# AdaLN block with memory-recurrent attention, forward and backward: the rows of a segment's out-projection and of its dH summed and turned off TensorE

## Chip, cores and metric

One Trainium2 chip, one core of it. The metric is the device time of one execution in microseconds (us), as the median of several runs. Engines in the profile: PE is TensorE (PEld its weight loads), DVE is VectorE, ACT is ScalarE, POOL is GpSimd, SP is SyncE, which issues most DMAs.

## What is computed

The output of the block and, by the vector-Jacobian product for `grad_out`, the gradients of its eleven differentiable inputs. Everything comes in as bfloat16. S = 2048 rows of D = 512; 32 heads of 128; 64 segments of 32 rows, each behind a memory of 8 rows; F = 1792.

```python
def _A_ref(x, mem0, Wq, Wk, Wv, Wo, seg_len):
    ...
    mem = mem0
    for s in range(n_seg):
        xs = x[:, s * seg_len:(s + 1) * seg_len, :].copy()
        h = jnp.concatenate([mem, xs], axis=1)          # 8 + 32 rows
        q = jnp.einsum('btd,dhe->bhte', h, Wq)
        ...                                             # k, v, masked softmax p
        o = jnp.einsum('bhqk,bhke->bhqe', p, v)
        o = jnp.einsum('bhte,hed->btd', o, Wo)
        mem = o[:, :M, :].copy()                        # M = 8: the next segment's memory
        outs.append(o[:, M:, :])
...
sa, ca, ga, sb, cb, gb = ...                            # from silu(c) @ w_mod
h = _layernorm(x, axis=-1) * (1 + ca) + sa
x = x + ga * _A_ref(h, A_mem0, A_Wq, A_Wk, A_Wv, A_Wo, A_seg_len)
h = _layernorm(x, axis=-1) * (1 + cb) + sb
x = x + gb * _B_ref(h, B_w_gate, B_w_up, B_w_down)      # (sigmoid(h Wg) * (h Wu)) Wd
```

A segment can't start its projections before the first 8 rows of the out-projection of the segment before it are there. Backward, a segment needs the first 8 rows of dH of the segment behind it. These are the two recurrences of the kernel.

## The kernel before

The instruction order on the engines follows the program text, which is written out by hand and pinned (`self.pin`). The stages, with their places in the span:

- Phase 2 (55 to 960 us): the forward recurrence, 64 segments s, in groups of four (s4 = s % 4), 14.0 to 14.9 us each.
- Phase 3 (968 to 1470 us): the gated unit, forward and backward, by tiles of 128 rows.
- Phase 4 (1475 to 2440 us): the backward recurrence, s from 63 to 0, 14.5 to 15.3 us each.
- Phase 5 (2440 us to the end): the weight gradients, products over all rows of all segments, and dx.

*The hand-over of phase 2.* A product in this kernel has D on the partitions. The out-projection of the first 32 rows of a segment (8 memory rows and 24 others) is `pair_mm` (L218 to L223): for each of 16 pairs of heads four matmuls side by side, each in its own 32-column tile of the array, so that `at_ps` holds four partial blocks, two partials of two column halves, [128, 256]. `split_pair` makes of it a bf16 part `hi` (ACT, L230) and the rest `lo` (DVE, L232); `sum_pair` (L235 to L242) adds the partial blocks and turns them with 8 small TensorE products against a 0/1 matrix (`foldhalf`), into `at_ft`, [128 of D, 4, 32 rows]. ACT copies its first 8 columns of each block into `hT_next` (L1022), which the next segment's K and Q projections (`pass_ps<-Wk,hT`, L257) read. The same rows also go to DRAM for phases 3 and 5: `store_rows` (L330) casts `at_ft` (DVE, `at_tb`, L333), and, one pass later through a list `later`, turns it on TensorE (`at_tp`, L337), copies it (DVE, `at_rb`, L339) and stores it (POOL DMA to `AOA`, L343).

*The last 8 rows of a segment.* They are collected for four segments (`TailRows`, tiles `ao_tail`) and projected in two pieces of 24 and 8 heads at s4 = 3 by `col_mm` (L215, products of 512 columns, `ao_tps`), then split (`fold_split`, L314 and L315, `ao_b_hi`, `ao_b_lo`), summed (`fold_sum`, L325, `ao_b_ft`) and stored in the same way.

*What stands between at_ps and the next projection.* Filler, put there by hand: passes of projections for rows that don't hang on the recurrence (`b_pieces`, slots "f1" and "f2", `pass_ps<-Wk,hb` and `Wq,hb`), a product that writes the causal mask into the next scores (`mask_mm`, L783), the tail's pieces (`tail.chunk`), and some products of the modulation.

*The hand-over of phase 4* is built alike: `dht_pairs` fills `dhq_ps` (64 products of 256 columns, then four with the folded rest `dST` of `dh_ps`, L223), `split_pair` makes `dh_hi` and `dh_lo`, `sum_pair` `dh_ft`, ACT copies into `dyT` (L1936), and the next segment's pass over WoT (`pass_ps<-WoT,dyT`, L257) reads it. The rows go to `DHA` through `dh_tb`, `dh_tp`, `dh_rb`. Its tail (`dh_tps`) has three operands of 32 heads, in pieces of (16, 24, 8, 8, 16, 8, 16) heads. `proj_b` (`pass_ps<-WoT,dyb`) is the filler, and `turn_b`, eight TensorE transposes of `RBd`, stands there at s4 = 1.

*PSUM.* Phase 2's pool has five shared slots (tag "p") and one more ("b", for the tail); phase 4's shared pool has six.

*Readers.* `load_x_rows` loads 128 rows of `AOA` or `DHA`/`DHB` for phases 3 and 5, by four or eight DMAs of whole 1 KB rows; in phase 5 `p5_second` (`dyrows`) and the load of `hrows` bring the memory rows of all segments, by two DMAs each.

## Time and profile before

| | |
|---|---|
| median of 3 runs | 2995.98 us |
| lowest, highest | 2993.12, 3000.86 us |
| profiled execution: span from first to last instruction (core 0) | 2991.0 us; no time of its own outside the span is recorded |
| granted TensorE clock, mean | 0.996 |
| PE, PEld busy | 2932.8 us (98%), 1839.9 us (62%) |
| DVE, ACT, POOL busy | 1612.4 us (54%), 1271.8 us (43%), 1197.2 us (40%) |

"Busy" counts the time in which at least one instruction of the engine runs; matmuls overlap, so the duration of one (273 ns for 256 columns) is longer than the distance to the next. In lines of a group, `out<-in xcount` gives tile names and the number of instructions; in a timeline, the columns are start and length in us, engine, line, operation, `out<-in` with shapes, and in brackets how long the engine stood before it and what ended that. L223 is line 223 of the kernel before.

### The profile page before, as it was taken

The numbers are of one execution on the slowest core, as the hardware profiler recorded it, in microseconds if no ns is written. First come the engines' busy times: TensorE is split into PE (matmuls) and PEld (weight loads), VectorE is DVE, ScalarE is ACT, GpSimd is POOL, SyncE is SP. The second block draws the span as 40 slices with busy tenths as digits, with TensorE's granted clock in tenths as the row PEclk, the third lists the DMA queues.
The fourth block names the chain that finished last, engine by engine and source line by source line (L and its number), as shares of the span: only waits on it lengthen the run. The fifth ranks groups of instructions, "written<-read, shape, count | busy, mean of one in ns | idle before, by whom it ended". The sixth has DMA issues, their size and how long they took to land.

```text
span 2991.0 us, 105890 instructions
## 1 busy us (share of the span) xinstructions
PE 2932.8 (98%) x43975; PEld 1839.9 (62%) x44049; DVE 1612.4 (54%) x3679; ACT 1271.8 (43%) x3057; POOL 1197.2 (40%) x2456
## 2 busy tenths in 40 slices
PE   6999999999999999999999999999999999999999
PEld 3666666666665544445677777777777754445454
DVE  5566656666655788833456665566566532222230
ACT  2555555555555533312355555555555520011111
POOL 2454555555545222221344444444444422333321
PEclk8999999999999999999999999999999999999999
DMA  9898888889889899998699999999999997766574
GB/s 310 222 223 211 214 217 217 213 214 215 217 218 277 211 230 226 229 290 278 200 251 251 251 253 243 250 250 250 255 255 250 254 281 245 242 207 214 178 245 144
DMA packets 836438, 703.05 MB, mean 235 GB/s; under 512 B 536643, under 2 KB 708851, under 8 KB 835061
## 3 DMA queue, kind: packets, MB, share of 16 engines
q1 hardware_dynamic: 710756, 486.09, 65.5%
q0 software_dynamic: 54640, 148.90, 15.7%
q10 hardware_dynamic: 70560, 61.28, 6.5%
q8 instruction: 347, 5.69, 0.8%
q14 instruction: 135, 1.10, 0.1%
HBM read 294.99 MB, written 276.35 MB: 191 GB/s over the span
## 4 chain that ended last, share of the span: by engine, by line
PE 87%; issue 5%; DMA 3%; DVE 2%; POOL 1%; ACT 1%; SPq 1%; DVEq 0%; POOLq 0%; ACTq 0%
PE pass_ps L257 14%; PE gps L2180 9%; PE dh_ps L215 8%; PE pass_ps L659 5%; PE g_ps L1810 5%; PE gps5o L2195 4%; PE dhq_ps L223 4%; PE at_ps L223 4%; PE mm L1291 3%; PE dh_tps L215 3%; PE gps L1470 3%; PE turn_ps L829 2%; PE mm L1266 2%; PE mm L1251 1%; PE tps L1727 1%
## 5 line engine op out<-in xcount | busy, mean ns | idle before, releaser
L2180 PE MATMUL gps<-rows,hrows 128*128 128x512 bf16 (+2 forms) x2125 | 415.6, 355 | 1.8
L2180 PEld LDWEIGHTS <-hrows 128*128 128x128 bf16 x2160 | 211.3, 98 | 204.5
L61 ACT ACTIVATE ot<-gps 128x512 bf16<-128x512 f32 (+3 forms) x75 | 41.3, 550 | 362.2 <-PE gps L2180 229.1
L1855 POOL COPY dOst<-RAd 96x512 bf16<-96x512 bf16 x128 | 75.3, 613 | 297.8 <-DVE RAd L63 297.8
L1038 POOL TENSOR_TENSOR Pst<-Pst,rden 120x1408 bf16<-120x1408 bf16 x63 | 159.9, 2538 | 77.8 <-issue 49.6
L659 PE MATMUL pass_ps<-Wv,hT 128*32 128x512 bf16 (+2 forms) x2304 | 187.2, 358 | 0.0
L63 DVE CAST ot<-gps 128x512 bf16<-128x512 f32 (+3 forms) x76 | 48.1, 633 | 247.0 <-PE gps L2180 169.9
L2184 POOL DMA_DIRECT2D out_dram<-ot x108 | 81.5, 755 | 249.1 <-DVE ot L63 141.9
L257 PEld LDWEIGHTS <-hT 128*32 128x32 bf16 x4096 | 114.8, 97 | 103.9 <-issue 5.7
L63 DVE CAST Vst<-pass_ps 96x512 bf16<-96x512 f32 x128 | 87.3, 682 | 107.0 <-ACT RBv L61 98.5
L215 PE MATMUL dh_ps<-WvT,dVT 128*32 128x512 bf16 x2048 | 133.3, 380 | 1.7
L659 PE MATMUL pass_ps<-Wv,hb 128*32 128x512 bf16 (+2 forms) x636 | 128.7, 353 | 0.0
L257 PE MATMUL pass_ps<-Wq,hT 128*32 128x512 bf16 x2048 | 123.9, 383 | 4.8 <-DMA Wq<-in_A_Wq_dram 4.8
L257 PE MATMUL pass_ps<-Wk,hT 128*32 128x512 bf16 x2048 | 123.2, 382 | 2.5 <-POOL hT L549 1.1
L223 PE MATMUL at_ps<-Wo,OT 128*32 128x256 bf16 x4096 | 123.9, 273 | 0.7 <-DMA Wo<-in_A_Wo_dram 0.6
L257 PE MATMUL pass_ps<-WoT,dyT 128*32 128x256 bf16 (+1 forms) x3072 | 122.5, 308 | 0.9 <-ACT dyT L1936 0.9
L223 PE MATMUL dhq_ps<-WqT,dQT 128*32 128x256 bf16 x4096 | 122.9, 273 | 0.0
L215 PE MATMUL dh_ps<-WkT,dKT 128*32 128x512 bf16 x2048 | 122.3, 380 | 0.0
L794 POOL DMA_DIRECT2D Vst<-RBv x192 | 99.9, 526 | 55.6 <-ACT ET L841 34.4
L2195 PE MATMUL gps5o<-WoT,rows 128*128 128x512 bf16 x548 | 120.6, 379 | 1.0 <-DMA rows<-OSR 0.4
L223 PEld LDWEIGHTS <-dQT 128*32 128x32 bf16 x4096 | 109.7, 97 | 15.8
L315 DVE TENSOR_TENSOR dST<-dh_ps,dST 128x512 bf16<-128x512 f32 x64 | 44.3, 692 | 129.9 <-ACT dST L314 129.9
(471 smaller groups left out, 6991.2 us busy)
## 6 DMA issues: line engine op xcount, KB each, us to landing
OSR<-Ost SPq DMA_DIRECT2D x64, 352.0 KB
OT<-OT SPq DMA_DIRECT2D x64, 352.0 KB
PS<-Pst SPq DMA_DIRECT2D x64, 352.0 KB
Pst_l<-PS SPq DMA_DIRECT2D x64, 352.0 KB
OT_l<-OT SPq DMA_DIRECT2D x64, 352.0 KB
DVR<-rows_x POOLq DMA_DIRECT2D x64, 352.0 KB, 6.3
DKR<-rows_x POOLq DMA_DIRECT2D x64, 352.0 KB, 5.7
DQR<-rows_x POOLq DMA_DIRECT2D x64, 352.0 KB, 3.4
```

The costliest lines, as they stand in the source:

```text
L63: return nc.vector.tensor_copy(out, in_)
L215: self.nc.tensor.matmul(ps[32 * j:32 * j + 32, :], lhsT=lhsT, rhs=w, start=(n < 4), stop=(n >= total - 4), tile_position=(0, 32 * j))
L223: nc.tensor.matmul(ps[32 * j:32 * j + 32, :], lhsT=x[k], rhs=w[k][:, 256 * d:256 * d + 256], start=(n == 0), stop=(n == total - 1), tile_p ...
L257: self.nc.tensor.matmul(ps[32 * j:32 * j + 32, :], lhsT=lhs(c), rhs=rhs, start=(c == 0), stop=(c == DC - 1), tile_position=(0, 32 * j))
L659: nc.tensor.matmul(ps[32 * j:32 * j + 32, o * E:(o + n) * E], lhsT=lhsT, rhs=wc[:, 3 * a + hl:3 * (a + n - 1) + hl + 1:3, :], start=(c == ...
L794: nc.gpsimd.dma_start(Vst[96 + 8 * j:104 + 8 * j, :], rb[32 * j + o:32 * j + o + 8, :])
L1038: nc.gpsimd.tensor_tensor(Pst[0:120, :, :], Pst[0:120, :, :], rden[:, :].unsqueeze(2).to_broadcast([120, G, 128]), op=ALU.mult)
L1291: nc.tensor.matmul(hp[:], lhsT=xT[:, fc, :], rhs=wT[:, fc, :], start=(n == 0), stop=(n == 2 * FC - 1))
L1470: nc.tensor.matmul(ps[:], lhsT=h2r[:, j, c * 128:(c + 1) * 128], rhs=xr[:, j, :], start=(j == 0), stop=(j == NT - 1))
L1810: nc.tensor.matmul(ps[:, j, 0:w], lhsT=lh[:, g * GW:(g + 1) * GW], rhs=rh[:, g * GW:g * GW + w], start=True, stop=True)
L2180: nc.tensor.matmul(ps[:, 0:ng * E], lhsT=hrows[:, tp_, c * 128:(c + 1) * 128], rhs=rows[:, tp_, 0:ng * E], start=(tp_ == 0), stop=(tp_ == ...
L2195: nc.tensor.matmul(pss[gg][:], lhsT=rows[:, t, gg * E:(gg + 1) * E], rhs=dyrows[:, t, :], start=(n == 0), stop=(n == NTP - 1))
```

## The change

The four partial blocks are laid out differently (`pair_mm`: partitions 0 to 63 hold the first operand's products, 64 to 127 the second's, and columns are dealt to the blocks in runs of 32, by a rearranged moving operand). `fold_rows` then adds them off TensorE: ACT copies the lower half to SBUF in f32, and two VectorE additions write `rows`, [128, 128] bf16, four column blocks by 32 rows. `turn_rows` turns the sixteen 32x32 blocks in one VectorE transpose, and a VectorE copy moves the 8 needed columns of each block into `hT_next` or `dyT_next`. `put_rows` stores `rows` to DRAM as they are, so the row scratch (`AOM`, `AOB`, `DHM`, `DHB`) holds the columns of D in another order. Its readers undo that: `load_x_rows` and `mem_rows` by DMAs of 256-byte pieces, `blocks` as a permuted access in a VectorE multiply, an ACT copy (`dhn5`, `hrows`) or a moving operand (`dy_rows`, 4 of 20 row tiles). `split_pair`, `sum_pair`, `fold_sum`, `store_rows` and the list `later` are gone.

The tails use `pair_mm` too (256 columns, pairs of heads), in pieces of (8, 24) at s4 = 2 and 3, and (16, 24, 8, 24, 8, 16) in phase 4; `ao_tps` takes a shared PSUM slot. The filler is dealt anew: in phase 2 each of s4 = 0, 1, 2 gets six steps of `b_pieces` (s4 = 2: four and a tail piece), all three mask products stand before the hand-over, and in phase 4 `turn_b` moves to the middle of the segment with s4 = 0.

Cut to its core (four leading spaces and some context taken off):

```diff
@@ -219,30 +218,36 @@
     nc = self.nc
     for j in range(4):
-        d, k = j // 2, j % 2
-        nc.tensor.matmul(ps[32 * j:32 * j + 32, :], lhsT=x[k], rhs=w[k][:, 256 * d:256 * d + 256], start=(n == 0),
-                         stop=(n == total - 1), tile_position=(0, 32 * j))
-def split_pair(self, pool, ps, name):
+        k, d = j // 2, j % 2
+        rhs = w[k].rearrange("p (b a h x) -> p h a b x", b=4, a=2, h=2)[:, d]
+        nc.tensor.matmul(ps[32 * j:32 * j + 32, :], lhsT=x[k], rhs=rhs, start=(n == 0), stop=(n == total - 1),
+                         tile_position=(0, 32 * j))
+def fold_rows(self, pool, ps, name):
     nc = self.nc
-    hi = pool.tile([128, 256], BF16, name=name + "_hi", tag="hi0", bufs=1)
-    nc.scalar.activation(hi[:], ps[:], AF.Copy)
-    lo = pool.tile([128, 256], BF16, name=name + "_lo", tag="lo0", bufs=1)
-    nc.vector.tensor_tensor(lo[:], ps[:], hi[:], op=ALU.subtract)
-    return hi, lo
-def sum_pair(self, psp, parts, name, tag, between=None):
-    ft = psp.tile([128, self.cfg.DC, 32], F32, name=name + "_ft", tag=tag)
-    for i in range(2):
-        if i and between is not None:
-            between()
-        for c in range(self.cfg.DC):
-            self.nc.tensor.matmul(ft[:, c, :], lhsT=parts[i][:, (c % 2) * 128:(c % 2) * 128 + 128],
-                                  rhs=self.foldhalf[:, c // 2, :], start=(i == 0 and c == 0), stop=(i == 1),
-                                  skip_group_check=True)
-    return ft
+    half = pool.tile([128, 256], F32, name=name + "_half", bufs=1)
+    nc.scalar.activation(half[64:128, :], ps[64:128, :], AF.Copy)
+    rows = pool.tile([128, 128], BF16, name=name + "_rows")
+    for a in range(2):
+        nc.vector.tensor_tensor(rows[64 * a:64 * a + 64, :], ps[0:64, 128 * a:128 * a + 128],
+                                half[64:128, 128 * a:128 * a + 128], op=ALU.add)
+    return rows
+def turn_rows(self, pool, rows, name, to):
+    nc = self.nc
+    t = pool.tile([128, self.cfg.DC, 32], BF16, name=name + "_turned")
+    nc.vector.transpose(t[:].rearrange("p c t -> p (c t)"), rows[:])
+    nc.vector.tensor_copy(to, t[:, :, 0:self.cfg.M])
+def put_rows(self, dram, rows):
+    self.nc.gpsimd.dma_start(dram.rearrange("i r y -> (i r) y"), rows[:])
+def blocks(self, ap, plain):
+    return ap.rearrange("p (b i x) -> p b i x" if plain else "p (i b x) -> p b i x", b=4, i=4)
...
@@ -315,41 +320,6 @@
-def fold_sum(self, psp, parts, name, tag, pair=()):
-def store_rows(self, psp, pool, ft, dram, name, tag, then=None):
-def pop_later(self):
...
@@ -361,8 +331,9 @@
     nc, T, M = self.nc, self.cfg.T, self.cfg.M
     q = q or nc.sync
     for s4 in range(4):
-        q.dma_start(dst[s4 * T:s4 * T + 24, :], a[4 * j + s4, M:32, :])
-        q.dma_start(dst[s4 * T + 24:(s4 + 1) * T, :], b[j, 8 * s4:8 * s4 + 8, :])
+        for r0, r1, src in ((0, 24, a[4 * j + s4, :, M:32, :]), (24, T, b[j, :, 8 * s4:8 * s4 + 8, :])):
+            q.dma_start(dst[s4 * T + r0:s4 * T + r1, :].rearrange("r (i y) -> r i y", i=4),
+                        src.rearrange("i r y -> r i y"))
...
@@ -630,8 +603,8 @@
             P = lambda x, a, n, eng: (lambda: proj_b(x, a, n, eng))
             T_ = lambda x: (lambda: turn_b(x))
-            return {(0, "f1"): [P("k", 0, 4, "dve")], (1, "f1"): [P("k", 4, 4, "dve")], (1, "f2"): [P("q", 0, 2, "act")],
-                    (2, "turn"): [T_("k")], (2, "f1"): [P("q", 2, 4, "dve")], (2, "f2"): [P("q", 6, 2, "act")],
+            return {(0, "f1"): [P("k", 0, 4, "dve")], (0, "f2"): [P("k", 4, 2, "act")], (1, "f1"): [P("k", 6, 2, "act")],
+                    (1, "f2"): [P("q", 0, 4, "dve")], (2, "turn"): [T_("k")], (2, "f1"): [P("q", 4, 4, "dve")],
                     (3, "turn"): [T_("q")]}
...
@@ -968,9 +934,6 @@
             den(2, or2)
             if s4 == 3:
                 p1(s // nseg_t + P1_AHEAD, 4)
-            early = s4 == 0 and len(self.later) > 1
-            if early:
-                self.pop_later()
             more = list(range(NP)) if s + 1 < NS else []
             if more:
                 mask_mm(more.pop(0))
@@ -980,16 +943,13 @@
             fill(s4, "turn")
             if s == NS - 1:
                 turn_v(2)
-            if more and s4 < 2:
+            if more:
                 mask_mm(more.pop(0))
             ott(0)
             if more:
                 mask_mm(more.pop(0))
             ott(1)
             ott(2)
-            if not early:
-                self.pop_later()
-            self.pop_later()
             if s == NS - 1:
                 nc.gpsimd.dma_start(self.w_down, io["B_w_down"].rearrange("(fc p) d -> p fc d", p=128))
@@ -1005,21 +965,21 @@
                 first_tile[6]()
             if s + 1 < NS:
                 tails_in("kq", s + 1)
-            parts = self.split_pair(sb2, at_ps, "at")
+            rows = self.fold_rows(sb2, at_ps, "at")
+            if hT_next is not None:
+                self.turn_rows(sb2, rows, "at", hT_next[:, :, 0:M])
+            self.put_rows(self.AOM[s + 1], rows)
             tail.collect(s4, [OT])
             nc.sync.dma_start(self.OT[s], gl3(OT))
             fill(s4, "f1")
             if s == NS - 1:
                 first_tile[7]()
-            if s4 == 3:
+            if s4 >= 2:
                 tail.chunk()
             if s == NS - 1:
                 turn_p(0)
                 first_tile[8]()
-            ft = self.sum_pair(psp, parts, "at", "p", (lambda: mask_mm(more.pop(0))) if more else None)
-            if hT_next is not None:
-                nc.scalar.activation(hT_next[:, :, 0:M], ft[:, :, 0:M], AF.Copy)
             fill(s4, "f2")
             if mod_r:
                 mod_r.pop()()()
...
@@ -1027,10 +987,7 @@
                 load, products = self.mod_rest(psp, sb2, mod_at.index(s + 1))
                 load()
                 mod_r.append(products)
-            if s4 == 3:
-                tail.chunk()
             tail.split()
-            self.store_rows(psp, sb2, ft, self.AOA[s + 1, 0:32, :], "at", "p")
             if s4 == nseg_t - 1:
                 tail.begin(s - nseg_t + 1, [Wo])
...
@@ -1322,7 +1278,8 @@
             def out():
                 nc.vector.tensor_tensor(da[:], dx1[:], ga_bc[:], op=ALU.mult)
                 nc.gpsimd.dma_start(self.DAROWS[r0:r1, :], da[:])
-                nc.vector.tensor_tensor(pr3[:], dx1[:], a_rows[:], op=ALU.mult)
+                nc.vector.tensor_tensor(self.blocks(pr3[:], True), self.blocks(dx1[:], True), self.blocks(a_rows, False),
+                                        op=ALU.mult)
...
@@ -1884,9 +1842,10 @@
             ds(0)
             ds(1)
             ds(2)
-            self.pop_later()
             dht(dVT, WvT, 0)
             dht(dVT, WvT, 1)
+            if s4 == 0 and s > 0:
+                turn_b(s // 4 - 1)()
             gv2 = grad_mm("dVT", dOst, Pst, 2)
             gr0 = grad_mm("dV", Pst, dOst, 0)
             gr1 = grad_mm("dV", Pst, dOst, 1)
@@ -1914,50 +1873,40 @@
             load_rows(Qst_t, self.QST, s - 1)
             for pi in range(NP):
                 grad_out("dKT", dKT, pi, "dve" if pi else "act", gks[pi])
-            self.pop_later()
             for pi in range(NP):
                 gq = grad_mm("dQT", Kst, dST, pi)
                 if pi == NP - 1:
                     load_rows(Kst_t, self.KST, s - 1)
                 grad_out("dQT", dQT, pi, "act", gq)
-            split = tail.split()
+            tail.split()
             for pi in range(NP):
                 dht(dKT, WkT, pi)
             dht(dVT, WvT, 2)
             parts = self.fold_split(sb2, dh_ps[0], "dh", dST)
-            pair = self.split_pair(sb2, dht_pairs(dQT, WqT), "dh")
+            rows = self.fold_rows(sb2, dht_pairs(dQT, WqT), "dh")
+            if dyT_next is not None:
+                self.turn_rows(sb2, rows, "dh", dyT_next[:, :, 0:M])
             tail.collect(s % nseg_t, [dVT, dKT, dQT])
             tail.chunk()
-            if split:
-                self.pop_later()
             store_rows_x(2)
-            ft = self.sum_pair(psp, pair, "dh", "p")
-            if dyT_next is not None:
-                nc.scalar.activation(dyT_next[:, :, 0:M], ft[:, :, 0:M], AF.Copy)
             g = s // 4
             if s >= NS - 2:
                 proj_b(g - 1, 3 - s4)()()
             elif s4 == 3 and g > 0:
                 b_rest.append(proj_b(g - 1, 1, 2))
-            elif s4 == 2:
-                tail.chunk()
-            elif s4 == 1 and g > 0:
-                turn_b(g - 1)()
             elif s4 == 0 and g > 1:
                 b_rest.append(proj_b(g - 2, 0, 2))
-            then = None
+            self.put_rows(self.DHM[s], rows)
             if s == 0:
-                def then(rb):
-                    nc.gpsimd.dma_start(io["out_2"].rearrange("o m (c x) -> (o m c) x", c=DC), rb[0:M * DC, :])
-            self.store_rows(psp, sb2, ft, self.DHA[s], "dh", "p", then)
+                for i in range(4):
+                    nc.gpsimd.dma_start(io["out_2"].rearrange("o m (b i x) -> i (o m) b x", b=4, i=4)[i],
+                                        rows[32 * i:32 * i + M, :].rearrange("m (b x) -> m b x", b=4))
             if s4 == 0:
                 tail.begin(s, [WvT, WkT, WqT])
         store_rows_x(0)
         last, i0 = self.pin(i0), len(self.traced())
-        tail.psb, tail.ptag = psp, "p"
-        tail.finish([lambda k=k: self.p5_products(range(4 * k, 4 * k + 4)) for k in range(3)],
-                    rxp.tile([128, G, 128], BF16, name="rows_x")[:].rearrange("p g x -> p (g x)"))
+        tail.psp, tail.tag = psp, "p"
+        tail.finish([lambda k=k: self.p5_products(range(4 * k, 4 * k + 4)) for k in range(3)])
         self.pin(i0, [mybir.EngineType.PE])
         self.pin_behind(i0, last, [mybir.EngineType.PE])
...
@@ -1999,16 +1948,24 @@
-            self.nc.tensor.matmul(ps[:], lhsT=src[0][:, src[1], gg * E:(gg + 1) * E], rhs=self.dyrows[:, t, :],
+            self.nc.tensor.matmul(ps[:], lhsT=src[0][:, src[1], gg * E:(gg + 1) * E], rhs=self.dy_rows(t),
-    nc, cfg, M, NS = self.nc, self.cfg, self.cfg.M, self.cfg.NS
-    Q = M // 2
+    NS = self.cfg.NS
+    self.mem_rows(self.dyrows, self.DHM[1:NS + 1])
+def dy_rows(self, t):
+    d = self.dyrows[:, t, :]
+    return self.blocks(d, False) if t < self.cfg.M // 2 else d
+def mem_rows(self, dst, src):
+    Q = self.cfg.M // 2
-        nc.sync.dma_start(self.dyrows[:, 0:Q, :].rearrange("(s k) t d -> k s t d", k=2)[k],
-                          self.DHA[1:NS + 1, Q * k:Q * k + Q, :])
+        for t in range(Q):
+            self.nc.sync.dma_start(dst[:, t, :].rearrange("(s k) (i y) -> k s i y", k=2, i=4)[k], src[:, :, Q * k + t, :])
...
@@ -2069,6 +2026,9 @@
             xh = sb1.tile([128, D], F32, name="xh5")
             nc.vector.tensor_scalar(xh[:], x0[:], mv[:, 0:1], rstd[:, 0:1], op0=ALU.subtract, op1=ALU.mult)
+            dhn = sb2.tile([128, D], BF16, name="dhn5")
+            nc.scalar.activation(self.blocks(dhn[:], True), self.blocks(dhb[:], False), AF.Copy)
+            dhb = dhn
             nc.tensor.matmul(acc_ps[:, :], lhsT=sel[:, 0, :], rhs=dhb[:], start=(j == 0), stop=False)
             pr = sb2.tile([128, D], BF16, name="pr5")
             nc.gpsimd.tensor_tensor(pr[:], dhb[:], xh[:], op=ALU.mult)
...
@@ -2261,17 +2222,18 @@
-    order = [(i, h) for i in range(self.n) for h in range(H)]
-    sizes = self.npieces if isinstance(self.npieces, tuple) else self.npieces * (len(order) // self.npieces,)
+    order = [(i, h) for i in range(self.n) for h in range(0, H, 2)]
+    sizes = [n // 2 for n in self.sizes]
-                st["ps"] = self.psb.tile([128, 512], F32, name=f"{self.name}_tps", tag=self.ptag)
+                st["ps"] = self.psp.tile([128, 256], F32, name=f"{self.name}_tps", tag=self.tag)
-                self.k.col_mm(st["ps"], tiles[i][:, h, :], ws[i][:, h, :], n, len(order))
+                self.k.pair_mm(st["ps"], [tiles[i][:, h + e, :] for e in range(2)], [ws[i][:, h + e, :] for e in range(2)],
+                               n, len(order))
...
@@ -2283,34 +2245,17 @@
+    if self.whole is not None:
+        (ps, s0), self.whole = self.whole, None
+        self.k.put_rows(self.dram[s0 // 4], self.k.fold_rows(self.pool, ps, self.name + "_b"))
+def finish(self, between=()):
...
```

99 lines of the change are left out of this document (26 added, 73 removed).

## Prediction

> **What bounds the kernel now.** The profile's page first: busy time of the engines, and the chain that ended last.
>
> ```profile
> PE 2932.8 (98%) x43975; PEld 1839.9 (62%) x44049; DVE 1612.4 (54%) x3679; ACT 1271.8 (43%) x3057; POOL 1197.2 (40%) x2456
> ...
> PE 87%; issue 5%; DMA 3%; DVE 2%; POOL 1%; ACT 1%; SPq 1%; DVEq 0%; POOLq 0%; ACTq 0%
> ```
>
> TensorE (PE) is busy in 98% of the span and makes 87% of the chain that ended last. So what counts is, segment by segment, how much PE work there is and how long PE lacks some. The change touches the hand-over from one segment to the next. The timeline of PE, ScalarE (ACT) and VectorE (DVE) around the end of a forward segment (s4 = 2) shows it (start, length, work):
>
> ```profile
> 601.05 0.61 PE L223 MATMUL at_ps<-Wo,OT 128*32 128x256 bf16 x16
> 601.49 1.04 PE L257 MATMUL pass_ps<-Wq,hb 128*32 128x512 bf16 x16
> 602.46 0.27 PE L242 MATMUL at_ft<-foldsel,at_hi 128*128 128x32 bf16 x4
> 602.57 0.31 PE L783 MATMUL st_ps<-maskT,ident 128*128 128x360 bf16 x1
> 602.72 0.25 PE L242 MATMUL at_ft<-foldsel,at_lo 128*128 128x32 bf16 x4
> 602.90 0.62 PE L257 MATMUL pass_ps<-Wq,hb 128*32 128x256 bf16 x16
> 603.35 0.61 PE L257 MATMUL pass_ps<-Wk,hT 128*32 128x512 bf16 x8
> ```
>
> ```profile
> 601.77 0.38 ACT L230 ACTIVATE at_hi<-at_ps 128x256 bf16<-128x256 f32 x1 [0.68 <-PE at_ps L223]
> 603.01 0.20 ACT L1022 ACTIVATE hT<-at_ft 128x32 bf16<-128x32 f32 x1 [0.85 <-PE at_ft L242]
> ```
>
> ```profile
> 601.12 0.42 DVE L63 COPY b_colsk<-turn_ps 128x512 bf16<-128x512 bf16 x1 [1.06 <-ACT b_colsk L61]
> 601.47 0.68 DVE L414 TENSOR_TENSOR h<-xh,sa_bc 128x512 bf16<-128x512 f32 x1
> 602.19 0.42 DVE L232 TENSOR_TENSOR at_lo<-at_ps,at_hi 128x256 bf16<-128x256 f32 x1
> 602.58 0.69 DVE L63 CAST RBq<-pass_ps 128x512 bf16<-128x512 f32 x1
> 603.24 0.45 DVE L333 CAST at_tb<-at_ft 128x128 bf16<-128x128 f32 x1
> ```
>
> PE never stands: filler passes (Wq,hb), the fold products and the mask product cover the chain at_ps, at_hi, at_lo, at_ft, hT. From the filler's start (601.49) to the next segment's first product on hT (603.35) are 1.86 us. The same stretch of the backward pass, dh_tps at 1943.96 to the dyT pass:
>
> ```profile
> 1943.96 1.04 PE L215 MATMUL dh_tps<-WqT,dh_tail 128*32 128x512 bf16 x16
> 1944.93 0.27 PE L242 MATMUL dh_ft<-foldsel,dh_hi 128*128 128x32 bf16 x4
> 1945.09 0.27 PE L242 MATMUL dh_ft<-foldsel,dh_lo 128*128 128x32 bf16 x4
> 1945.28 0.62 PE L257 MATMUL pass_ps<-WoT,dyb 128*32 128x512 bf16 x8
> 1945.73 0.82 PE L257 MATMUL pass_ps<-WoT,dyT 128*32 128x512 bf16 x12
> ```
>
> 1.77 us. I call this stretch the window; segments run in groups of four. Counted from the start of the last product before it (0.1 us earlier) the windows of a group are, forward, s4 = 0 to 3: 1.93, 1.93, 1.97, 2.40 (8.23 together); backward, s4 = 3 to 0: 2.01, 2.24, 1.87, 1.86 (7.98).
>
> **The PE work taken away is no gain in the window.** By their rows the fold products and row transposes are busy 116 us, overlapped (at_ft 34, dh_ft 34, the tp's 35, the tails' sums 14). But inside the windows they were cover. After the change the window holds filler alone: by the order of the changed kernel, 48 column-tiled products of 256 columns or as much. 32 tiled products of 512 take 1.73 us on PE (54.1 ns each) and 64 of 256 take 1.75 (27.5), so this is 1.31 us. If the new chain is longer, PE waits for it, and its length alone sets the window.
>
> **The new chain, step by step, from the filler's start.** ACT begins 0.28 behind it (601.77 - 601.49; 0.23 to 0.28 over segments). `half` is 64x256 f32: 0.38, as at_hi, since partitions run side by side. ACT to DVE 0.035. Two adds of 64x128: DVE on f32 PSUM takes 692, 558 and 425 ns for 512, 384 and 256 columns, a line of 158 + 1.04 per column, so 0.29 each; a 64x128 cast in the trace has 0.27. They start on other partitions; where the trace has that (RBv), the second starts 0.03 after the first's end, while neighbours on the same partitions overlap by 0.08. I take +0.03. The transpose is not in the trace. Its neighbours are the 128x128 bf16 copies L339 (0.215 to 0.225), one element per cycle by the line (0.29) and the strided cast L333 (0.45). I take 0.30, between 0.22 and 0.45, as a transposing unit should hardly beat the plain line; +0.03 before it, for it waits on DVE's own result. The copy of 4x8 columns: 0.15 (a 24-column SBUF copy) to 0.17 (a 32-column one), take 0.16, +0.03 before it. To PE 0.05 to 0.08. Sum: 0.28 + 0.38 + 0.035 + 0.29 + 0.03 + 0.29 + 0.03 + 0.30 + 0.03 + 0.16 + 0.06 = 1.89 forward, against 1.86 shown; 1.84 backward (ACT after 0.23), against 1.77. PE idles 1.89 - 1.31, about 0.55 us per segment (70 us in all), where before it did the folds.
>
> The Trainium skill (page "VectorE: DVE Perf Modes", section "The three transpose paths") gives 311 ns for VectorE's turn of 128x128 bf16 in 32x32 blocks; by it the chain would be 0.01 longer. No run here shows it yet.
>
> The ends: short row values with overlap make the chain 0.28 + 0.38 + 0.035 + 0.47 + 0.22 + 0.15 + 0.05 = 1.58; long ones (transpose 0.45, 0.06 for each hop on DVE) 2.13. There are 127 hand-overs, so 0.1 us of chain is 12.7 us.
>
> **Windows per group.** With 1.99 from the last product: forward 4 x 1.99 = 7.96, -0.27 (s4 = 3 gives it: its 2.40 held fold products and tail chunks); s4 = 2 may lose 0.05, as DVE's h is ahead of the adds. Backward 4 x 1.95 = 7.80, -0.18.
>
> **Outside the windows, where PE is full.** Forward per group: s4 = 0 loses two transposes and ao_b_ft (-0.36), s4 = 1 a transpose and a tail bit (-0.12); s4 = 2 and 3 get a third mask product back (0.16 to 0.20, no longer between folds) and, with ao_tps holding a PSUM slot, about 0.1 of wait: +0.10, +0.20. Sum -0.18. Backward: turn_b's eight transposes come out of a window into full PE time, +0.45, four dh_tp go at 0.06 each: +0.22. Tails turn from 512-column to paired 256-column products: same PE time (54.1 against 2 x 27.5).
>
> **Ends.** The end of the forward pass (963 to 968 us) has 0.52 + 0.46 + 0.54 us of idle in the tail's fold and row transposes, with their work 2.5 us; most goes. The first two backward windows (2.29) become 1.95. The last tail is shorter. Together -3.5.
>
> **Hidden.** Loads in 256-byte pieces (SP), the 16 dhn5 and 4 hrows copies on ACT (0.6 us each by the 128x512 rows; ACT is 11% busy from 2440 us on), permuted VectorE multiplies in phase 3, POOL's put_rows in place of the old row stores (0.56 us of issue each, as before). In the trace PE takes the products of these rows 6 us or more after they are ready; uncovered, the sixteen copies cost at most 10 us. The filler's evacuations on DVE now stand behind the turn (up to 1.8 us later); the next pass needs their PSUM only after 1.9 us of products.
>
> **Sum.** Forward 16 x (-0.27 - 0.18) = -7.2; backward 16 x (-0.18 + 0.22) = +0.6; ends -3.5: -10. The profiled execution's span is 2991.0, 5 us under the median of 2996.0 and 2 under the fastest run, so it stands for an ordinary run with some us around it; the change of span is put on the median: 2996 - 10 = 2986.
>
> **Rivals.**
> *Shorter chain:* adds overlap as same-partition neighbours do (-0.11), transpose at the copies' 0.22: chain 1.70, -0.19 x 127 = -24 more, about 2962. For it: bf16 copies at 0.22. Against: the RBv rows.
> *Longer chain:* five dependent DVE steps of about 0.16 fixed time each replace two ACT and one DVE step. With transpose 0.45 and hops at 0.06, 2.13: +0.24 x 127 = +30, about 3016; it decides from a chain of about 2.04 on, 0.15 over the forecast's, where the 19 us have turned -10 into +9. That an unfilled chain stops PE shows at s = 60: before at_ft and again before at_lo
>
> ```profile
> 931.27 0.27 PE L242 MATMUL at_ft<-foldsel,at_hi 128*128 128x32 bf16 x4 [0.55 <-ACT at_hi L230]
> 931.73 0.26 PE L242 MATMUL at_ft<-foldsel,at_lo 128*128 128x32 bf16 x4 [0.19 <-DVE at_lo L232]
> ```
>
> The Trainium skill (page "Advanced Engine Details and Errata", section "TRN2 Errata") says that VectorE and ScalarE show the memory's latency as a bubble between instructions, and advises large tiles; it speaks against five small steps. The trace agrees in the 158 ns of the line, and disagrees in the 0.08 by which neighbours overlap.
> *Pair products slowed:* the moving operand is now read in runs of 32 columns. Rows with runs of 128 (L257, Wk) and with one run (L215, dKT) both have 379 ns and equal spacing, 49.4, so I expect no price. 10% on 64 products of 27.5 ns would be 0.18 us x 127 = +22, plus 3 in tails: 3011. The Trainium skill (same page, section "Memory Cachelines") says that any non-contiguous pattern slows matmuls significantly; it says so of PSUM, whose side stays contiguous here, and no row of before has runs of 32.
> *Nothing left over:* the chain is 0.05 to 0.1 longer and eats the gain: 2990 to 3000.
>
> **Chances.** Forecast's cell (2977 to 2995) 0.38, shorter chain 0.18, nothing left over 0.13, longer chain 0.21, slowed products 0.10. A measurement of this kernel tells 0.3% (9 us) from no change; of the forecast's cell 0.22 lies beyond that. Faster 0.22 + 0.18 = 0.40, same 0.16 + 0.13 = 0.29, slower 0.21 + 0.10 = 0.31. The forecast hangs on the chain to within 0.15 us, so signs are mixed; alone its cell is 2977 to 2995. The range runs from the shorter chain's 2962 to 3014, between the two slower cases' prices, and leaves out about half of each outer case.
>
> **What would show it.** Right: PE idle of 0.5 to 0.6 us before pass_ps on hT and dyT, released by the DVE copy, in every segment; busy PE 96%; half 0.38, transpose about 0.3; pair products at 27.5 ns spacing; windows of 1.95 to 2.0 everywhere. Wrong: transpose rows at 0.22 or over 0.4, adds held by other DVE work, wider spacing of L223, or new waits in the body (PSUM slots, masks).

## The result, and the profile after

| | before | after |
|---|---|---|
| median (4 runs each) | 2997.61 us | 3022.74 us |
| span of the profiled execution | 2991.0 us | 3019.8 us |
| PE busy | 2932.8 us (98%) | 2897.2 us (96%) |

The ratio is 1.0087, 95% interval 1.0072 to 1.0101: 25 us slower, where the forecast was 10 us faster. The page's first part, and who PE waited for (engine, line, releaser: us in total, times, longest):

```profile
PE 2897.2 (96%) x44657; PEld 1853.8 (61%) x44657; DVE 1606.0 (53%) x3771; ACT 1251.2 (41%) x2951; POOL 1180.9 (39%) x2414
```

```profile
PE pass_ps L262 <- DVE hT L242: 31.7, 47, 1.8
PE pass_ps L262 <- DVE dyT L242: 23.8, 58, 1.7
...
PE tp L1085 <- DVE w_downT L63: 6.8, 1, 6.8
...
PE dh_tps L223 <- issue: 5.5, 6, 1.9
```

The first two lines are the idle time that the prediction named: in 105 of the 126 hand-overs PE waits for VectorE's last copy, 55.5 us in all (about 70 forecast). The third and fourth were not in the forecast; "issue" is time in which PE waited for nothing that the profile shows. The window of s4 = 2 shown before, now on PE, ACT and DVE:

```profile
610.99 1.04 PE L262 MATMUL pass_ps<-Wq,hb 128*32 128x512 bf16 x16
611.86 0.61 PE L223 MATMUL ao_tps<-Wo,ao_tail 128*32 128x256 bf16 x16
...
613.31 1.05 PE L262 MATMUL pass_ps<-Wk,hT 128*32 128x512 bf16 x16 [0.84 <-DVE hT L242]
```

```profile
611.28 0.38 ACT L230 ACTIVATE at_half<-at_ps 64x256 f32<-64x256 f32 x1 [0.72 <-PE at_ps L223]
```

```profile
611.69 0.58 DVE L233 TENSOR_TENSOR at_rows<-at_ps,at_half 64x128 bf16<-64x128 f32 x2
612.30 0.31 DVE L241 STREAM_TRANSPOSE at_turned<-at_rows 128x128 bf16<-128x128 bf16 x1
612.65 0.52 DVE L242 COPY hT<-at_turned 128x32 bf16<-128x32 bf16 x1
```

The chain runs as drawn, from the filler's start (610.99) to the next pass (613.31): 2.32 us. In the other forward segments the copy takes 0.175, as here one segment earlier:

```profile
598.30 0.18 DVE L242 COPY hT<-at_turned 128x32 bf16<-128x32 bf16 x1
```

Counted as in the prediction, from the start of the last product before, windows are 2.08 (s4 = 0, 1, 3) and 2.41 (s4 = 2). Backward, the window on PE and DVE:

```profile
1947.60 1.05 PE L223 MATMUL dh_tps<-WkT,dh_tail 128*32 128x256 bf16 x32
1948.47 0.61 PE L223 MATMUL dh_tps<-WqT,dh_tail 128*32 128x256 bf16 x16
1949.42 1.81 PE L262 MATMUL pass_ps<-WoT,dyT 128*32 128x512 bf16 x44 [0.34 <-DVE dyT L242]
```

```profile
1949.19 0.17 DVE L242 COPY dyT<-dh_turned 128x32 bf16<-128x32 bf16 x1
```

1.82 us, or 1.93 from the last product, in all four kinds of segment. So where did 28.8 us of span come from? The starts of the first projections of each segment cut both timelines into stages. Difference to the profiled execution of before in us, with the experiments below (phase 2 and phase 4: 63 hand-overs each; "to phase 4" holds the end of phase 2 and phase 3; "rest" is what follows the last hand-over of phase 4). In the runs of these experiments the median of the kernel before was 2995.7 to 3001.2 us; each ratio is to the kernel before in the same set of runs.

| kernel | start | phase 2 | to phase 4 | phase 4 | rest | median | ratio to before (95%) |
|---|---|---|---|---|---|---|---|
| changed | +0.8 | +10.9 | +4.5 | +10.1 | +2.3 | 3022.7 | 1.0072 to 1.0101 |
| e1, before, 8 loads | +1.2 | +0.3 | +6.1 | +1.1 | +1.1 | 3002.1 | 0.9999 to 1.0031 |
| e2, mask in window | +0.8 | +9.7 | +12.0 | +8.9 | +4.5 | 3024.1 | 1.0060 to 1.0104 |
| e3, turn_b in window | +0.0 | +8.8 | +3.2 | +1.4 | +2.2 | 3014.0 | 1.0042 to 1.0076 |
| e4, half copy cut | +0.7 | +12.3 | +4.9 | +7.3 | +3.8 | 3025.8 | 1.0080 to 1.0124 |
| e5, copy on ACT | +0.6 | +6.2 | +11.9 | +14.8 | +2.3 | 3014.6 | 1.0045 to 1.0087 |
| e6, four loads | +0.7 | +9.9 | +5.8 | +6.3 | +1.7 | 3018.1 | 1.0059 to 1.0089 |
| e7, five edits | +0.1 | +8.6 | +8.0 | +0.8 | +7.4 | 3016.4 | 1.0047 to 1.0079 |
| e8, before, halved tails | -0.1 | +4.1 | +2.8 | +34.9 | +3.5 | 3032.0 | 1.0090 to 1.0145 |
| e9, wide dH tail | +1.1 | +10.4 | +5.7 | +8.4 | +4.2 | 3021.1 | 1.0059 to 1.0089 |
| e10, half in two tiles | +0.4 | +13.9 | +5.0 | +11.3 | +2.0 | 3027.4 | 1.0079 to 1.0114 |
| e11, four edits | -0.4 | +9.5 | +4.7 | +3.5 | +5.7 | 3015.9 | 1.0042 to 1.0072 |
| e12, GpSimd adds | +0.1 | +5.1 | +3.6 | +19.1 | +6.2 | 3027.8 | 1.0073 to 1.0120 |
| e13, edits, fold early | +0.7 | +7.7 | +4.9 | -7.8 | +3.8 | 3001.1 | 1.0004 to 1.0026 |
| e14, backward only | +1.0 | +0.7 | +1.0 | -8.9 | +1.8 | 2990.9 | 0.9963 to 0.9983 |

Most segments of a kind (the same s4) are equally long to 0.05 us. By the medians of the four kinds a forward group grew from 57.16 to 57.74 us, and a backward group from 59.10 to 59.13, hardly at all. The +10.1 of phase 4 sits in single segments that are longer than the median of their kind: these excesses sum to 6.4 us before and to 16.6 in the changed kernel. Of a segment, what lies outside its window is called the body below.

One execution's stages scatter: e2 and e5 lost 7 us more in phase 3, where PE waited 4.6 and 3.9 us for a transposing DMA (dgT). So an edit is read from the stage that it touches, and its time from the runs.

### The profile page after: what moved, and what is told of

It is laid out like the page before. It is cut to its first block, busy times and chain, and to the rows that moved or that the text cites. A ratio compares the mean times of both kernels' runs of the same rounds, so it can differ in the third digit from the quotient of the medians.

```text
span 3019.8 us, 107073 instructions
## 1 busy us (share of the span) xinstructions
PE 2897.2 (96%) x44657; PEld 1853.8 (61%) x44657; DVE 1606.0 (53%) x3771; ACT 1251.2 (41%) x2951; POOL 1180.9 (39%) x2414
## 5 line engine op out<-in xcount | busy, mean ns | idle before, releaser
L61 ACT ACTIVATE RAd<-pass_ps 128x256 bf16<-128x256 f32 x128 | 48.4, 383 | 182.1 <-PE pass_ps L262 182.1
L262 PEld LDWEIGHTS <-dyT 128*32 128x32 bf16 x3072 | 76.2, 97 | 77.4 <-DVE dyT L242 47.8
```

The source lines that it names most:

```text
L61: return nc.scalar.activation(out, in_, AF.Copy)
L262: self.nc.tensor.matmul(ps[32 * j:32 * j + 32, :], lhsT=lhs(c), rhs=rhs, start=(c == 0), stop=(c == DC - 1), tile_position=(0, 32 * j))
```

## Experiments

**Chain and windows.** In e4 and e10 ScalarE's copy is cut in two, so that VectorE may start earlier.

```diff
-nc.scalar.activation(half[64:128, :], ps[64:128, :], AF.Copy)
+for a in range(2):
+    nc.scalar.activation(half[64:128, 128 * a:128 * a + 128], ps[64:128, 128 * a:128 * a + 128], AF.Copy)
```

> The changed kernel with ScalarE's copy of the lower half cut in two of 64x128, so that VectorE's first addition starts after the first. Theory, the chain sets every window: by the rows (ScalarE 64x256 0.378, 128x32 0.198, so 64x128 about 0.275) the second addition ends 0.89 us after ScalarE's start instead of 0.99; the windows go from 2.08 to 1.98 (forward) and from 1.93 to 1.83 (backward), and the time falls by 126 x 0.10 = 12 us, to about 3010. Rival: something else ends the windows (filler, the x columns of hT, PSUM); then they stay within 0.03 and the time within 4 us of the changed kernel.

Measured 3025.8 us (ratio 1.0080 to 1.0124). e10 gives each piece its own tile:

> As the run with ScalarE's half copy cut in two, but with a tile of its own for each piece: there the first addition waited for both pieces (ScalarE 0.44 us for the two, VectorE's first addition after them). Theory, the chain sets the windows: the first addition now starts after 0.27 + 0.03, the second ends 0.10 us earlier than in the changed kernel; windows 1.98 forward (2.31 at s4 = 2) and 1.83 backward, and the time 126 x 0.10 = 12 us lower, about 3011. Rival: the windows stay within 0.03 us, since something else ends them.

Both edits lengthened the chain: with two tiles, too, the first addition began only after the second piece (0.032 us after its end, in both runs), as this window of e10 on ACT and DVE shows.

```profile
1951.94 0.44 ACT L231 ACTIVATE dh_half<-dhq_ps 64x128 f32<-64x128 f32 x2 [1.20 <-PE dhq_ps L223]
```

```profile
1952.41 0.60 DVE L234 TENSOR_TENSOR dh_rows<-dhq_ps,dh_half 64x128 bf16<-64x128 f32 x2 [0.94 <-ACT dh_half L231]
```

Why (both engines read one PSUM tile) was not tried. So the gain did not come, but the theory was tested all the same, from the other side: the chain grew by 0.06 us and the windows went to 2.14 and 2.00, in every segment but the forward ones of s4 = 2. The chain sets the windows.

**The copy that takes 0.51.** e5 changes the last step at s4 = 2:

```diff
-nc.vector.tensor_copy(to, t[:, :, 0:M])
+nc.scalar.activation(to, t[:, :, 0:M], AF.Copy)      # at s4 == 2
```

> The changed kernel with the last step of the forward chain (128x32, turned rows into hT) on ScalarE instead of VectorE at s4 = 2, where this VectorE copy takes 0.51 us instead of 0.175. Theory: the VectorE copy is held while GpSimd runs its own three bf16 copies at that moment (kT from b_colsk); on ScalarE it takes about 0.20 with 0.035 ahead of it, the windows at s4 = 2 fall from 2.41 to about 2.11, and the time by 13 x 0.3 = 4 us, to about 3019. Rival: the copy waits for something else that it writes or reads (the hT buffer, the x columns that GpSimd puts beside it); then ScalarE's copy ends as late, and the windows at s4 = 2 stay at 2.4.

The windows of s4 = 2 fell to 2.13, phase 2 from +10.9 to +6.2, the median by 8 us (by the ratios 6; 4 were expected, and the rest is not explained). ScalarE's copy takes 0.228 us in all sixteen. What GpSimd did in the window of the changed kernel:

```profile
612.49 0.64 POOL L65 COPY kT<-b_colsk 128x192 bf16<-128x192 bf16 x3
613.07 0.64 POOL L65 COPY qT<-b_colsq 128x192 bf16<-128x192 bf16 x3
```

VectorE's copy (612.65 to 613.17) ends 0.04 us after GpSimd's first three do (613.13), and so it does in all 12 segments in which it takes 0.51. In three of the sixteen segments with s4 = 2 no GpSimd copy runs beside it, and it takes 0.175. In e4, where it begins 0.06 us later, it takes 0.45 and ends at the same place; that is why the windows of s4 = 2 stayed there. It is not every time the third copy that it waits for: in one segment, and in 14 of e6, it took 0.30 and ended 0.1 us after the first. The Trainium skill (page "SBUF — State Buffer", section "SBUF: two separate sides") says that VectorE's copies in a two-port mode and GpSimd share a port pair under an exclusive lock. The trace agrees with a wait for GpSimd: 0.51 us beside its copies, 0.175 without them, 0.228 on ScalarE. Whether this copy runs in a two-port mode no run shows.

**The third mask product.** e2:

```diff
-                ott(0)
-                if more:
-                    mask_mm(more.pop(0))
+                ott(0)
...
+                if more:
+                    mask_mm(more.pop(0))
                 fill(s4, "f2")
```

> The changed kernel with the third mask product of every forward segment put back between at_ps and the next projection (ahead of the second filler). Theory: PE stands about 0.5 us in each hand-over, so the product costs nothing there; the windows stay at 2.08 (2.41 at s4 = 2) and each segment loses 0.16 to 0.2 us of body: 10 to 12 us less than the changed kernel, about 3011 (ratio 1.0045 to 1.006 to the kernel before). Rival: the longer bodies come from waits for PSUM slots and not from this product; then segments are as long as in the changed kernel within 0.05 us, and the time stays within 4 us of it.

No gain came: 1.2 us less in phase 2, the same time. The rival had the time right, but the waits for PSUM slots that it names do not show. The windows stayed at 2.08, and ahead of at_ps nothing was gained: at_ps starts 10.37, 10.61 and 11.1 us after the segment's first projection at s4 = 0, 2 and 3, with the third mask product ahead of it and without. Segments of s4 = 2 did lose 0.16 us, but by VectorE's copy, which took 0.35 instead of 0.51 there; those of s4 = 1 grew by 0.11, as products of the modulation slid into them. A new line says what PE waits for instead, 15 times of 17 at s4 = 2:

```profile
PE at_ps L223 <- DVE OT L63: 3.3, 17, 0.3
```

With the mask product gone from the body, PE waits there for VectorE's OT, the turned attention output. The body ahead of at_ps isn't bounded by PE alone.

**turn_b.** e3 puts it back:

```diff
-                if s4 == 0 and s > 0:
-                    turn_b(s // 4 - 1)()
...
+                elif s4 == 1 and g > 0:
+                    turn_b(g - 1)()
```

> The changed kernel with the eight transposes of turn_b back in the hand-over of the backward segments with s4 = 1. Theory: PE's idle time there (0.5 us) takes their 0.45 us, windows stay at 1.93, and a group of four segments loses 0.45 us of body, and 0.24 more where the next products waited for VectorE's copy of RBd or the turned columns: 7 to 10 us less than the changed kernel, 3012 to 3016. Rival: the transposes and their evacuation push the chain itself (VectorE's turn or the next pass late); then the window at s4 = 1 grows to 2.2 or more and the time stays within 3 us of the changed kernel.

As expected, but for windows at s4 = 1 of 2.06 instead of 1.93: segments of s4 = 0 lose 0.69 us, phase 4 went from +10.1 to +1.4 and the median fell by 9 us.

**Instruction waits.** Phase 4 of the changed kernel has gaps of 0.8 to 1.9 us in the middle of work, in a few segments only. One of them:

```profile
1877.60 0.38 PE L223 MATMUL dh_tps<-WkT,dh_tail 128*32 128x256 bf16 x5 [1.94 <-issue]
```

PE waited for nothing but its own queue. The changed tails have twice as many instructions for the same PE time by spacing. e8 does that alone, to the kernel before:

```diff
-self.k.col_mm(st["ps"], tiles[i][:, h, :], ws[i][:, h, :], n, len(order))
+for c in range(2):      # 256 columns each, start only for the first
+    self.k.nc.tensor.matmul(st["ps"][j:j + 32, 256 * c:256 * c + 256], lhsT=tiles[i][:, h, :], ...)
```

> The kernel before with every tail product (512 columns) issued as two of 256 columns: the same PE time by spacing (54.1 against 2 x 27.5 ns), 2048 more matmuls and 2048 more weight loads, as in the changed kernel's tails. Theory: more PE instructions in the backward pass make PE wait for instructions (the waits that the profile calls issue): these rise from 2 us to 5 to 10 in phase 4, and the time by 4 to 8 us (ratio 1.001 to 1.003). Rival: those stalls come from the changed order of DMAs, not from the number of instructions; they stay under 3 us and the ratio is within 0.001 of 1.

The theory held, but its size was some five times too small: 34.9 us in phase 4, 36 us in the median (ratio 1.0090 to 1.0145). The array's own time is not the reason: 26 of the 63 segments are as long as before to 0.05 us, and 34.6 us come from the others. Its waits in phase 4, then those of the kernel before:

```profile
PE pass_ps L257 <- issue: 7.2, 9, 2.2
PE g_ps L1810 <- issue: 4.1, 5, 1.4
PE turn_ps L1683 <- issue: 2.3, 2, 2.0
...
PE dp_ps L1787 <- issue: 1.4, 1, 1.4
```

```profile
PE dp_ps L1795 <- issue: 1.7, 1, 1.7
...
PE dh_tps L215 <- issue: 0.4, 1, 0.4
PE pass_ps L257 <- issue: 0.4, 1, 0.4
```

Instructions come by DMA. The queue that the profile calls instruction carries packets of 16 KB, some 2.5 per segment of phase 4. The page's line of the kernel before, and of e8:

```profile
q8 instruction: 347, 5.69, 0.8%
```

```profile
q8 instruction: 363, 5.95, 0.8%
```

Sixteen packets more for 4096 more instructions of PE: 64 bytes each, 256 in a packet. In e8 PE stood over 0.6 us 17 times in phase 4 (20.4 us; before once, 1.8 us), and in 16 of them such a packet had landed 1.2 to 1.75 us before PE went on. In the changed kernel all 12 waits called issue in phase 4 ended so, though only a tenth of the stage's time lies that far behind a packet; the segments with such gaps hold 11.3 of its 16.6 us of excess (3.1 of 6.4 before). Gaps account for some 23 of the 34.9 us in e8; the rest was not separated. A packet is 128 products with their weight loads: 3.5 us of PE time at 27.5 ns, 6.9 us at 54.1. It takes 1.07 us (median) to arrive, and PE goes on some 1.5 us after it has landed. Why a few packets come too late and most do not stays open. The DMA engines are full in phase 4 (busy share 1.0 before and in e8), and no run changed that. The Trainium skill (page "Runtime: NRT & Kernel Launch", section "Instruction fetch mechanics") says that instructions stream in 16 KiB blocks by the sequencer's own DMA queue, which is mostly hidden. The blocks agree; hidden they were not.

e9 takes the dH tail back to 512 columns and folds it off TensorE:

```diff
+nc.scalar.activation(half[64:128, :], ps[64:128, :], AF.Copy)                               # 64x512
+nc.vector.tensor_tensor(half[0:64, :], ps[0:64, :], half[64:128, :], op=ALU.add)
+for i in range(4):      # 32x128 each
+    nc.vector.tensor_tensor(rows[32 * i:32 * i + 32, :]..., half[0:32, block i], half[32:64, block i], op=ALU.add)
```

> The changed kernel with the dH tail's products back at 512 columns (1536 matmuls and 1536 weight loads fewer, the same PE time), folded off TensorE: ScalarE copies 64x512, VectorE adds 64x512 once and 32x128 four times. Theory, late instructions: with fewer PE instructions the stalls over 0.6 us in phase 4 that end some 1.5 us after a 16 KB packet of the instruction queue (five, 6.6 us, in the changed kernel; one, 1.8 us, in the kernel before; thirteen in the kernel before with halved tail products) fall to two at most, and the time by 5 to 8 us, to 3015 to 3018. Rival: the stalls follow the order of the DMAs, not the number of instructions; four or more stay and the time is within 3 us of 3022.7.

The stalls went (one gap over 0.6 us is left, and that is a wait for GpSimd; no wait called issue is left in phase 4), but the time did not. Segments of s4 = 3 are 0.67 us longer, and a wait of 0.4 us in each of them is new; the rest of the 0.67 was not separated:

```profile
PE dhq_ps L223 <- DVE dST L332: 5.6, 14, 0.4
```

VectorE's dST now stands behind the longer fold. All kernels bear out what the number of instructions does: the excess of phase 4 is 10.2 to 21.3 us in the eight with the changed kernel's paired dH tail, and 0.9 to 7.5 in the seven with products of 512 columns there (the kernel before, e1, e9 and e11 to e14).

**The start of phase 3.** In the changed kernel PE stands 6.8 us there; VectorE waits 7.6 us for rows (2.5 before), and the evacuation of w_downT is queued behind. First before, then after:

```profile
970.95 0.69 DVE L1153 TENSOR_TENSOR t<-Wv 128x512 f32<-128x512 bf16 x1 [2.50 <-DMA Wv<-AOA]
```

```profile
985.55 0.69 DVE L1109 TENSOR_TENSOR t<-Wv 128x512 f32<-128x512 bf16 x1 [7.56 <-DMA Wv<-in_grad_out_dram]
```

e1 gives the kernel before eight loads per tile, and e6 the changed kernel four:

```diff
-q.dma_start(a_rows[32 * i:32 * i + 32, :], self.AOA[4 * j + i + 1, M:M + T, :])
+q.dma_start(a_rows[32 * i:32 * i + 24, :], self.AOA[4 * j + i + 1, M:32, :])
+q.dma_start(a_rows[32 * i + 24:32 * i + 32, :], self.AOA[4 * j + i + 1, 32:M + T, :])
```

> The kernel before, with one edit: the rows of a tile of phase 3 are loaded by eight DMAs (24 and 8 rows of 1 KB for each segment) instead of four of 32 rows. In the changed kernel VectorE waits 7.6 us (2.5 before) for the load of the second tile at the start of phase 3, and PE then stands 6.8 us. Theory, number of DMAs: the eight DMAs stand on SP's queue behind the last stores of phase 2 and each is issued about 2 us after the one before it; so the wait and a PE gap of 4 to 7 us come up here too, and the time is 4 to 7 us over the kernel before (ratio 1.0013 to 1.0023). Rival, size of the pieces: the changed kernel's 256-byte pieces make the loads slow; here pieces are still 1 KB, so no new PE gap and a ratio of 1.000 within 0.001.

> The changed kernel with the 40 rows of a segment in one scratch tensor, so that a tile of phase 3 is loaded by four DMAs (256-byte pieces) instead of eight; the tail's rows are stored by four DMAs on GpSimd's queue instead of one. Theory, number of DMAs: the PE gap at the first w_downT transposes (6.8 us in the changed kernel, 2.8 in the kernel before with eight DMAs, none with four) falls below 2 us; the time falls by about 5 us. Rival, pieces of 256 bytes: the gap stays at 4 us or more.

e1 has a gap of 2.8 us at that place (4 to 7 expected), and its ratio is not clear of 1; e6 still has 6.7. So the number of loads is at most a part of the cause. In e6 as in the kernel before, VectorE gets the rows 9 to 10 us after the last of the four loads was issued, with the DMA engines over 90% busy (8 MB in 22 us). Counted from the first projection of the last segment, that load is issued 17.1 us on in e6 (15.4 before), and VectorE is free for the rows after 19.7 us (22.1 before), as the folds at the end of phase 2 are gone. These two make 4.1 of the 4.9 us that VectorE waits longer. So the rival's sign, a gap of 4 us or more, came, but 256-byte pieces can have only part in it; how much they add was not settled.

**All edits.** Two runs took edits together and met new waits. e7 (turn_b, copy, four loads, the cut half copy, mask at s4 = 2):

> The changed kernel with turn_b back in the window at s4 = 1, the copy into hT on ScalarE at s4 = 2, ScalarE's half copy cut in two, four loads per tile in phase 3, and at s4 = 2 alone the third mask product in the window. Theory: the gains add, 9 + 5 + 12 + 4 + 2 = 32 us off the changed kernel, about 2990, 0.2% under the kernel before (ratio 0.996 to 1.000). Rival: PE's instruction waits and other stalls outside the windows (up to 10 us more in the changed kernels' backward pass than before) stay and the parts overlap: 3000 to 3005.

It gave 3016.4 us, beyond the rival too. e11 (wide tail, cut half copy, turn_b, copy) gave 3015.9; in both the cut copy had made the chain longer, and e11 kept e9's wait for dST (segments of s4 = 3 are 0.75 us longer than in the changed kernel).

> The changed kernel with four edits: half copy in two tiles, wide dH tail, turn_b in the window at s4 = 1, copy into hT on ScalarE at s4 = 2. Theory: the gains add, 12 + 6 + 8 + 4 = 30 us, about 2993, level with the kernel before or up to 0.3% under it (ratio 0.996 to 1.000). Rival: the windows with turn_b (0.45 us more on PE) no longer shorten with the chain, and instruction stalls come back elsewhere; about 3003 (ratio 1.002).

e12 leaves the half copy whole, and the last additions of the wide tail to GpSimd:

> The changed kernel with turn_b in the window at s4 = 1, the copy into hT on ScalarE and the third mask product in the window at s4 = 2, and the dH tail at 512 columns; of the tail's fold VectorE does only the one addition of 64x512 (0.69 us, as the kernel before), ScalarE moves the lower sums (two copies of 32x256), GpSimd adds four blocks of 32x128. Theory: the instruction stalls stay away as in the run with the wide tail, without the 0.4 us for which dhq_ps waited there for VectorE's dST; with turn_b (-9) and the copy (-5) the time is about 3000, level with the kernel before (ratio 0.999 to 1.003), the rest being the forward windows, 0.15 us longer than before, and the late load at the start of phase 3. Rival: GpSimd's additions stand ahead of the row loads on its queue and make PE wait elsewhere in phase 4; 3006 or more (ratio 1.003 to 1.006).

3027.8 us: dhq_ps waited 15.3 us for ScalarE's and 6.2 us for VectorE's dST, since ScalarE's second small copy waited for GpSimd and held up what was queued behind it. e13 moves the wide tail's fold (VectorE again) ahead of the dQT products:

```diff
+                tail.split()
                 for pi in range(NP):
                     gq = grad_mm("dQT", Kst, dST, pi)
...
-                tail.split()
```

> The changed kernel with turn_b in the window at s4 = 1, the copy into hT on ScalarE and the third mask product in the window at s4 = 2, and the dH tail at 512 columns, folded on VectorE as in the run with the wide tail, but ahead of the dQT products, where VectorE has 2.4 us of idle time. Theory, side changes: no instruction stalls in phase 4, no wait of dhq_ps for dST, windows of 1.93 to 2.05; phase 4 ends 5 to 8 us earlier than in the kernel before against its start, phase 2 5 us later, the start of phase 3 4 us later: 2998 to 3003 (ratio 0.999 to 1.002). Rival, the fold itself: phase 4 is no shorter than before, or dst waits stay; 3008 or more (ratio over 1.003).

3001.1 us, as expected; phase 4 is 7.8 us shorter than before, so the fold off TensorE pays there. Phase 2 is still 7.7 longer. e14 therefore keeps the forward pass of before:

> The kernel before up to phase 4 (fold and row turns on TensorE, rows stored as before), with the backward pass and phase 5 of the run with the early fold. Theory: the fold off TensorE gains in the backward pass alone, where the filler's end and the chain lie closer and PE does not wait for the turned rows' second releaser; phase 4 is 8 us shorter than before, phases 2 and 3 as before, phase 5 up to 4 us longer by one instruction stall at its start: 2991 to 2995 where the kernel before has 2997 (ratio 0.998 to 0.9995). Rival: the gain in phase 4 was one of that run's layout of DMAs or instructions, and goes with another program in front; ratio 1.000 to 1.003.

2990.9 us, ratio 0.9973 (0.9963 to 0.9983): faster than both kernels, and a little more so than expected. The gain in phase 4 (8.9 us) came with another program in front, so the rival fails. A backward group is 58.58 us by its medians (59.10 before). That the forward pass loses by a second releaser was not tried by itself.

## Why the prediction was wrong

Four steps failed, each in its own place: the forward windows (11 us worse than forecast), what lies outside the hand-overs (11), instruction waits, which were left at zero (10), and the forward bodies (6). The backward group came out as forecast.

- **Chain: nearly right.** Measured: half 0.378 (0.38 forecast), additions 0.283 (0.29) with 0.014 between (0.03), transpose 0.311 (0.30), copy 0.175 (0.16), hops on VectorE 0.035 (0.03). The mis-sized term is the last, forward: from the copy's end to PE's first product 0.147 (0.06), with a step of PE's queue of 0.05 us ahead of the weight load; backward, without that step, it is 0.056. So windows are 2.08, not 1.99, and 1.93, as against 1.95.
- **"The copy 0.15 to 0.17, take 0.16"** failed at s4 = 2: 0.51, worth some 5 us. The prediction looked for VectorE's own work ahead of the chain (h, which ended in time), not at GpSimd.
- **Windows per group.** Forecast -0.27 and -0.18; measured 8.65 - 8.23 = +0.42 forward and 7.72 - 7.98 = -0.26 backward. Over all hand-overs +6.5 and -5.3 us (the first two backward windows went from 2.29 to 1.93). Forward this is the largest miss, 0.69 per group, by the two terms above.
- **"Outside the windows, where PE is full".** Forward -0.18 was forecast, +0.17 per group came (+0.59 with the windows). Two premises failed: PE is not the only bound there, as e2 shows, so that a product taken out frees nothing where PE then waits for OT; and the bodies of s4 = 2 and 3, which got a third mask product, grew by 0.20 and 0.31, not by 0.10 and 0.20. Backward +0.29 came for +0.22. With the windows that is +0.03 per group, where +0.04 was forecast, partly by luck: turn_b cost 0.69 and not 0.45, since dKT's products came 0.24 later too, and the rest gave back more than forecast.
- **"Same PE time (54.1 against 2 x 27.5)"** was true of the array and false of the kernel: the price of the tails' instruction count was left at zero. Waits called issue grew from 2.6 to 8.2 us in phase 4 and just behind it, and the excess of single segments by 10.2 us, of which 8.2 lie in segments where PE went on some 1.5 us after a packet of instructions had landed. e8 shows what this price can become.
- **"Ends" and "Hidden".** Forecast -3.5; the start, the end of phase 2 with phase 3, and the rest together came to +7.6. The 3 us at the end of phase 2 were gained (phase 3's first products start 18.6 us after the last segment's first projection, before 21.6) and more than paid back: the first products on w_downT start after 38.1 us, before 33.5. The load of the second tile was just in time before, and what was late next was not named. Of the +2.3 of the rest, 1.9 is one more wait called issue. How much the 256-byte pieces cost stays open.
- **Rivals.** The slower side was forecast by a longer chain (2.13) or slowed pair products. The chain came longer only forward, and by other terms: a sum of misses elsewhere made the time, so that the 3022.7 us lie near the longer chain's 3016 by chance. Slowed pair products did not come: at_ps takes 1.66 us and dhq_ps 1.76 from first to last start in both kernels, though the moving operand is read in runs of 32. The Trainium skill (page "VectorE: DVE Perf Modes", section "The three transpose paths") had 311 ns for the transpose; the trace has 0.311.

## What to carry to other kernels

An edit that keeps the array's time but doubles the number of instructions has a price of its own: look for idle time that the profile calls issue, and for segments that are longer than others of their kind. Work moved out of a covered wait is only paid back if the stretch that it leaves or enters is bounded by the same engine; read each stage's last wait before giving it a sign. And an edit with two mirror halves can be right in one: here, in e13, phase 2 lost 8 us and phase 4 gained 8.

## What was unexpected in the hardware

- PE waiting for its instructions, in e8 in gaps of 0.6 to 2.2 us of which 16 of 17 ended 1.2 to 1.75 us after a 16 KB packet of the instruction queue had landed.
- A VectorE copy of 128x32 bf16 from SBUF to SBUF of 0.30 to 0.51 us beside GpSimd copies, 0.175 without them; the additions from PSUM and the 32x32 transpose (0.311, every time within 5 ns) did not stretch, though 42 of the forward additions and 14 of the transposes ran beside a GpSimd copy.
